# A new hand-written order for the first three batches of an attention and MLP kernel, with one output transfer fewer

## The chip, the cores and the metric

The kernel runs on one core of one Trainium2 chip. The metric is the device time of one execution in microseconds (us). Three runs of the kernel before took 201.86 to 201.91 us, median 201.90 us. The core has five engines with a queue each: PE (TensorE, matrix products), DVE (VectorE), ACT (ScalarE), POOL (GpSimd) and SP (SyncE, which here only issues DMA transfers). ACT and POOL issue a few transfers too.

## The reference

For 8 batches with 8 heads, 512 tokens and 32 state rows of 64 numbers each, attention runs both ways between tokens `x` and rows `state`. The result then goes through two dense layers with a leaky ReLU between them.

```python
scores = scale * x @ state.T;  a  = softmax(scores);  xread = a @ state     # tokens read the states
scores2 = scale * state @ x.T; a2 = softmax(scores2); sread = a2 @ x        # states read the tokens
x = concat([xread, sread], axis=2)            # 8 * 544 rows of 512
out = leaky_relu(x @ w_in, 0.01) @ w_out      # 512 -> 2048 -> 512
```

## The kernel before, in words

The eight batches are worked one behind another, and parts of three of them are in flight at any time. For a batch b these steps occur:

- The tokens are loaded in float32 (`load_x`, tile `xl`, a single buffer), cast to bfloat16 (`cast_x`, tile `xb`) and transposed (tile `xT`). For batch 1 the loads (two tiles `x1`, issued by POOL) are cast on DVE by `cast_x1(u)` and transposed on PE by `turn(u)`, one half u at a time. From batch 2 on `a_xt_dma` transposes by a DMA that SP issues.
- `a_scores` (L223) is a group of eight small products on PE, which needs `xT` and a transposed state. Its result feeds a chain on DVE and ACT: maximum (`a_top`), its spread over rows (`a_rows`), subtraction (`a_less`), exponential (`a_exp`), reciprocal and product (`a_probs`), which gives `aT`. `a_exp2`, `a_max2` and `a_probs2` do the other softmax, `a_a2t` transposes its result by DMA.
- `a_m` (called by `m_make`, and by `mk` in the strings below) multiplies the state by `w_in`, a quarter of the columns at a time, and `m_take` or `ev` copies the result out of PSUM to tile `M`.
- `ff1` (called `ff(j)` or `f.j`) makes one sixteenth of the hidden layer on PE. Its ReLU on ACT (`relu.pop(j)()`, or `r.j`) writes it to `hT`. Two PSUM buffers with the tag `ph` alternate between these, so a later product waits for an earlier ReLU.
- The second layer of batch 0 is cut into `piece(0, h0, i, jq, part=...)`: row group i, quarter jq of the hidden layer, one matmul for each of up to four parts. The pieces of i = 2 and 3 sum in the tile `wide` (named `pyw` in the trace). From batch 1 on the second layer is a fast matrix product with seven products in place of eight (`Fast`), cut into units of two matmuls (`before.run(1)`, or `u`). It needs sums of hidden tiles, made on DVE (`f.sums`, or `sb`, `sn`), and sums of weights, made by `weights_sum` on DVE and POOL into four tiles `tw`.

Nothing is scheduled by a planner. The program runs under `tc.manual_schedule`, so each engine executes its instructions in the order in which the source calls them. For batches 0, 1 and the beginning of 2 the calls stand one by one (L1115 to L1269). For batch 2's own stretch the order is a string of short names, `FIRST` (L1358), which `stretch` (L1270) reads from left to right. Batches 3 to 6 share the string `ORDER`, which stays as it is, and batch 7 has a loop.

A call only fixes the order inside each engine. Waits come from the data: a semaphore wait is put ahead of an instruction whose input or buffer is not ready. The transfers of SP and ACT use eight DMA semaphores in rotation, in the order in which the source calls them, so each transfer also waits until the eighth one before it has landed. At the end of the kernel SP waits for these semaphores one after another, from number 0 to number 7 (shown under L1578), and the cores' engines meet in a barrier.

The names that the change and the prediction touch: on POOL `weights_sum(3, 4, 8)`, `(0, 4, 8)`, `(1, 0, 4)` (L734) and the four casts of batch 3's tokens (L114); on SP the load of batch 3's tokens (L108) and their transposition (L207); on PE the `turn`s (L1095), the pieces (L697), `a_scores` of batches 2 and 3 (L223) and `f.3` of batch 2 (L412); and the output rows of batch 4 in `Batch.done` (L847).

Of the kernel before, what the change touches and what calls it, by code (L numbers as in the profile page):

```python
# [10 lines left out]
B, H, S, D = 8, 8, 512, 64  # L11
# [19 lines left out]
def kernel(  # L31
# [9 lines left out]
    nc = tc.nc  # L41
# [68 lines left out]
    def open_xb(b):  # L110
        xs[b] = xpool.tile([P, NT, H, D] if b < 2 else [P, 2, NT, NK, D], BF16, name="xb", tag="xb")

    def cast_x(b, h0, h1, copy):
        copy(  # L114
            xs[b][:, h0 // NK, :, h0 % NK:h0 % NK + h1 - h0].rearrange("p t h d -> p h t d"),
            xl[b][:, h0:h1].rearrange("p h (t d) -> p h t d", t=NT),
        )
# [59 lines left out]
    def load_state(i, ks=range(NK)):  # L177
        lo, hi = groups[i]
        for k in ks:
            for g in range(2):  # L180
                nc.sync.dma_start(
                    stf[i][NS * k:NS * (k + 1), :, D * g:D * (g + 1)],
                    state[lo:hi, 2 * k + g].rearrange("b n d -> n b d"),
                )
# [10 lines left out]
    def a_open(a, b):  # L195
        a.b = b
        a.xb = xs[b]
        a.xT = att.tile([P, NT, NK, P] if b < 2 else [P, 2, NT, 2, P], BF16, name="xT", tag="xT")
# [108 lines left out]
    def a_exp2(a, g):  # L307
        if g == 0:
            a.e2 = att.tile([P, 2, S], BF16, name="e2", tag="e2", bufs=3)
            a.r2 = att.tile([P, 2], FP32, name="r2", tag="r2", bufs=3)  # L310
        nc.scalar.activation(  # L311
            out=a.e2[:, g], in_=a.sc[:, g, :], func=AF.Exp,
            bias=a.m2[:, g:g + 1], accum_out=a.r2[:, g:g + 1],
        )
# [376 lines left out]
    def piece(b, hT, i, jq, bank=None, copy=SCA, part=range(4)):  # L691
        if jq == 0:
            y = ys[b, i] = Y()
            y.py = psum.tile([P, DM], FP32, name="py", tag="py")[:] if bank is None else bank
        y = ys[b, i]
        for j in (4 * jq + v for v in part):
            nc.tensor.matmul(  # L697
                y.py, lhsT=hT[:, j, P * i:P * (i + 1)], rhs=w_out_bf[:, j, :],
                start=(j == 0), stop=(j == 15),
            )  # L700
        if jq == 3 and copy is not None:
            y_store(b, i, copy)
# [20 lines left out]
    def weights_open():  # L723
        for tag in ("xf0", "xf1", "x10", "x11"):
            tw.append(consts.tile([P, NM, HC], BF16, name=f"tw_{tag}", tag=tag))
# [60 lines left out]
    class Batch:  # L786
# [44 lines left out]
        def done(self, n, bank, copy=SCA):  # L831
            f = self.f
            if n in (1, 6, 5, 7):
                f.save(n, bank, copy)
            if n == 2:
                f.join(self.yo(0)[:, :, :HC], bank, 1)
                if self.b == B - 1:
                    self.out(0, slice(0, HC))
            elif n == 7:
                nc.gpsimd.tensor_tensor(  # L840
                    out=self.yo(1)[:, :, HC:], in0=f.sv[7][:], in1=f.sv[5][:], op=ALU.add
                )
                if self.b == B - 1:
                    self.out(1, slice(HC, DM))
            elif n == 3:
                f.join(self.yo(0)[:, :, HC:], bank, 6)
                for i in range(2) if self.b in (2, 3, 4) else (None,):  # L847
                    self.out(0, slice(HC if self.b == B - 1 else 0, DM), i)
            elif n == 4:
                f.join(self.yo(1)[:, :, :HC], bank, 7)  # L850
                self.out(1)
# [238 lines left out]
    def turn(u):  # L1090
        pt[u] = psum.tile([P, NT, 2, P], BF16, name="pxt2", tag="ph")
        for t in range(NT):
            for v in range(2):
                h = NK * u + 2 * v
                nc.tensor.transpose(  # L1095
                    pt[u][:, t, v, :], a1.xb[:, t, h:h + 2, :].rearrange("p h d -> p (h d)"), ident[:]
                )

    def cast_x1(u):
        VEC(  # L1100
            a1.xb[:, :, NK * u:NK * (u + 1)].rearrange("p t h d -> p h t d"),
            x1[u][:].rearrange("p h (t d) -> p h t d", t=NT),
        )

    def m_make(a, c, tag):
        pmt[a.b, c] = a_m(a, c, tag)
# [8 lines left out]
    h1 = hpool.tile([P, 16, S], BF16, name="hT", tag="hT")  # L1115
    before = Batch(1, h1)
    wide = psum.tile([P, 2, DM], FP32, name="pyw", tag="big", bufs=1)
    a_exp2(a0, 0)
    piece(0, h0, 0, 0)
    load_state(0)  # L1120
    cast_x1(0)
    turn(0)
    cast_x1(1)
    piece(0, h0, 2, 0, bank=wide[:, 0])
    piece(0, h0, 1, 0)
    a_exp2(a0, 1)
    VEC(a1.xT[:, :, 0:2, :], pt[0][:])
    turn(1)
    VEC(a1.xT[:, :, 2:4, :], pt[1][:])
    piece(0, h0, 3, 0, bank=wide[:, 1])  # L1130
    m_make(a1, 1, "ph")
    open_xb(2)
    weights_open()
    a_scores(a1)
    m_take(a1, 1, 0, SCA)
    m_take(a1, 1, 1, VEC)
    a_top(a1)
    piece(0, h0, 0, 1, copy=None, part=(0, 1))
    piece(0, h0, 1, 1, copy=None, part=(0, 1))
    piece(0, h0, 2, 1, copy=None, part=(0, 1))  # L1140
    piece(0, h0, 1, 1, copy=None, part=(2, 3))
    m_make(a1, 2, "ph")
    m_take(a1, 2, 0, SCA)
    m_take(a1, 2, 1, SCA)
    weights_sum(2, 0, 4, nc.gpsimd)
    weights_sum(0, 0, 4, nc.gpsimd)
    state_t(0)
    piece(0, h0, 0, 1, copy=None, part=(2, 3))
    piece(0, h0, 2, 1, copy=None, part=(2, 3))
    piece(0, h0, 3, 1, copy=None, part=(0, 1))  # L1150
    m_make(a1, 3, "ph")
    piece(0, h0, 2, 2, copy=None, part=(0, 1))
    piece(0, h0, 1, 2, copy=None, part=(0, 1))
    a_rows(a1)
    a_less(a1)
    a_exp(a1)
# [2 lines left out]
    cast_x(2, 4, 5, POO)  # L1159
    cast_x(2, 5, 6, POO)  # L1160
    cast_x(2, 6, 7, POO)
    a_open(a2, 2)
    cast_x(2, 7, 8, POO)
    a_probs(a1, 0)
    piece(0, h0, 0, 2, copy=None, part=(0, 1))
    a_xt_dma(a2, slice(1, 2))
    piece(0, h0, 0, 2, copy=None, part=(2, 3))
    piece(0, h0, 3, 1, copy=None, part=(2, 3))
    piece(0, h0, 2, 2, copy=None, part=(2, 3))
    piece(0, h0, 3, 2, copy=None, part=(0, 1))  # L1170
    a_xt_dma(a2, slice(0, 1))
    a_exp2(a1, 0)
    a_probs(a1, 1)
    piece(0, h0, 1, 2, copy=None, part=(2, 3))
    piece(0, h0, 3, 2, copy=None, part=(2, 3))
    load_x(3, nc.sync)
    open_xb(3)
    piece(0, h0, 3, 3, copy=None, part=(0, 1))
    weights_sum(2, 4, 8)
    weights_sum(1, 4, 8)  # L1180
    weights_sum(3, 4, 8, nc.gpsimd)
    weights_sum(0, 4, 8, nc.gpsimd)
    weights_sum(1, 0, 4, nc.gpsimd)
    cast_x(3, 0, 2, POO)
    a_exp2(a1, 1)
    m_take(a1, 3, 0, SCA)
    cast_x(3, 2, 4, POO)
    cast_x(3, 4, 6, POO)
    piece(0, h0, 2, 3, copy=None, part=(0, 1))
    m_make(a2, 0, "sc")  # L1190
    m_take(a1, 3, 1, SCA)
    ff(0)
    ff(1)
    m_take(a2, 0, 0, VEC)
    relu.pop(0)()
    piece(0, h0, 3, 3, copy=None, part=(2, 3))
    m_take(a2, 0, 1, VEC)
    relu.pop(1)()
    ff(2)
    piece(0, h0, 2, 3, copy=None, part=(2, 3))  # L1200
    ff(3)
    relu.pop(2)()
    a_a2t(a0)
    a_scores(a2)
    cast_x(3, 6, 8, POO)
    relu.pop(3)()
    y_store(0, 2, SCA)
    y_store(0, 3, SCA)
    piece(0, h0, 0, 3, copy=None, part=(0, 1))
    piece(0, h0, 0, 3, copy=None, part=(2, 3))  # L1210
    a_top(a2)
    a_open(att_of[3], 3)
    a_rows(a2)
    y_store(0, 0, SCA)
    ff(4)
    a_less(a2)
    ff(5)
# [5 lines left out]
    piece(0, h0, 1, 3, copy=None, part=(0, 1))  # L1223
    ff(9)
    a_a2t(a1)
    a_xt_dma(att_of[3])
    a_max2(a2)
    relu.pop(6)()
    piece(0, h0, 1, 3, copy=None, part=(2, 3))
    relu.pop(8)()  # L1230
    relu.pop(9)()
# [1 line left out]
    a_exp(a2)  # L1233
    a_probs(a2, 0)
    before.run(1)
    a_probs2(a0)
    ff(10, "big")
    before.run(1)
    ff(12)
    relu.pop(10)()  # L1240
    before.run(1)
    ff(13)
    before.run(1)
    before.run(1)
    before.run(1)
    load_state(1, range(2, 4))
    before.f.sums(0, 0, 4)
    a_probs(a2, 1)
    relu.pop(12)()
    relu.pop(13)()  # L1250
    a_exp2(a2, 0)
    a_exp2(a2, 1)
    ff(14)
    relu.pop(14)()
    ff(15)
    relu.pop(15)()
    before.run(1)
    before.run(1)
    before.run(1)
    before.run(1)  # L1260
# [1 line left out]
    m_make(a2, 2, "sc")  # L1262
    m_make(a2, 1, "big")
    m_take(a2, 2, 0, SCA)
    m_take(a2, 1, 0, VEC)
    m_take(a2, 2, 1, SCA)
    before.run(1)
# [2 lines left out]
    def stretch(b, hT, before, now, order):  # L1270
# [85 lines left out]
    )  # L1356

    FIRST = (  # L1358
# [7 lines left out]
    )  # L1366

    for b in range(2, B):
# [4 lines left out]
        if b < B - 1:  # L1373
            stretch(b, hT, before, now, FIRST if b == 2 else ORDER)
            before = now
# [207 lines left out]
```

## Time and profile before

| | |
|---|---|
| median of three runs | 201.90 us (201.86 to 201.91) |
| the profiled execution, its time | 201.93 us |
| its span, first to last instruction | 200.2 us |
| PE busy | 193.9 us (97%), 2090 matmuls |
| DVE, ACT, POOL busy | 164.7, 150.5, 62.2 us |
| TensorE clock granted | 1.00 throughout |
| DMA | 28.02 MB, mean 140 GB/s |

The time of the execution is 1.7 us more than the span: the work around the first and the last instruction. In the profile "busy" of PE is modelled, since matmuls are pipelined. A row of the timeline gives the start, the duration, the engine, the line, the operation, the tiles (output, then inputs) and, in brackets, how long the engine stood idle before it and what ended that. SPq is the issuing of transfers by SP. "DMA to landing" is the time from the start of the issue until the last of the 16 DMA engines has reported the transfer as done.

### The profile page before, as it was taken

Reading aid. Unit: us, or ns where it says so; the run is one execution under the profiler, and the core shown is the slowest. Engines: PE = TensorE matmul, PEld = TensorE weight load, DVE = VectorE, ACT = ScalarE, POOL = GpSimd, SP = SyncE. Lnnn points to the kernel's source line nnn. Section 1 sums busy time; section 2 is a strip of 40 time slices with the busy share of each in tenths; the row PEclk is TensorE's granted clock in tenths of the full one; section 3 lists DMA queues with packets and bytes.
Section 4 is the critical chain, followed back from the end, with each engine's and each line's share of the span. In section 5 each row is a group of like instructions: output and inputs, shape, how many; then the busy total and the mean of one; then the engine's idle time right before and its main releaser. Section 6 shows DMA issues by size and latency. Waiting matters only on the chain.

```text
span 200.2 us, 5119 instructions
## 1 busy us (share of the span) xinstructions
PE 193.9 (97%) x2090; PEld 136.5 (68%) x2090; DVE 164.7 (82%) x283; ACT 150.5 (75%) x287; POOL 62.2 (31%) x90
## 2 busy tenths in 40 slices
PE   7999899999999999999999999999999999999992
PEld 2566544345677667776777777767777788799881
DVE  2676579799998989998999899999899977995622
ACT  3478728699778749996999679987999778767610
POOL 8483266591046013310422040400040024004350
PEclk9999999999999999999999999999999999999999
DMA  6999997999543994734393613080023402210035
GB/s 201 210 207 264 238 296 128 183 282 248 146 147 70 303 285 91 228 151 115 68 246 114 177 34 72 7 258 0 3 83 127 82 0 108 105 56 0 7 98 164
DMA packets 39992, 28.02 MB, mean 140 GB/s; under 512 B 25440, under 2 KB 36832, under 8 KB 39968
## 3 DMA queue, kind: packets, MB, share of 16 engines
q1 hardware_dynamic: 34176, 20.35, 38.1%
q0 software_dynamic: 4960, 6.55, 16.1%
q10 hardware_dynamic: 832, 0.79, 1.2%
q8 instruction: 16, 0.26, 0.6%
q14 instruction: 8, 0.07, 0.1%
HBM read 17.30 MB, written 8.91 MB: 131 GB/s over the span
## 4 chain that ended last, share of the span: by engine, by line
PE 89%; DMA 6%; DVE 1%; POOL 1%; ACT 0%; issue 0%
PE yq L768 43%; PE ph L412 18%; DMA x<-in_x_dram 6%; PE pm L391 4%; PE pyw L697 4%; PE py L697 3%; PE pf L490 3%; PE pl L658 3%; PE yu L768 3%; PE pspin L143 2%; PE pl L579 2%; PE psn L357 1%; PE sc L223 1%; PE phw L425 1%; PE pxt L1095 1%; PE yz L768 0%
## 5 line engine op out<-in xcount | busy, mean ns | idle before, releaser
L418 ACT ACTIVATE hT<-ph 128x512 bf16<-128x512 f32 x84 | 48.9, 609 | 12.3 <-PE ph L412 12.1
L768 PEld LDWEIGHTS <-su 128*128 128x128 bf16 x480 | 46.2, 98 | 12.6 <-ACT hT L418 0.4
L412 PE MATMUL ph<-aT,M 128*128 128x512 bf16 x168 | 47.6, 379 | 0.0
L768 PEld LDWEIGHTS <-hT 128*128 128x128 bf16 x336 | 32.3, 98 | 11.7 <-issue 2.5
L768 PE MATMUL yq<-tw_xf,su 128*128 128x256 bf16 x224 | 30.9, 273 | 0.0
L768 PE MATMUL yq<-w_out_bf,hT 128*128 128x256 bf16 x224 | 29.2, 273 | 0.0
L840 POOL TENSOR_TENSOR yo<-sv,sv 128x512 f32<-128x512 f32 x7 | 9.3, 1329 | 42.6 <-ACT e L311 38.2
L412 PEld LDWEIGHTS <-M 128*128 128x128 bf16 x168 | 16.0, 98 | 7.9 <-issue 1.9
L757 DVE TENSOR_TENSOR su<-hT 128x1024 bf16<-128x1024 bf16 x28 | 19.0, 682 | 2.7 <-ACT hT L418 2.7
L1288 ACT CAST M<-pm 128x512 bf16<-128x512 f32 x31 | 17.3, 599 | 1.4 <-PE pm L391 1.4
L114 POOL CAST xb<-xl 128x512 bf16<-128x512 f32 (+1 forms) x24 | 13.5, 604 | 12.6 <-DMA xl<-in_x_dram 12.6
L777 ACT COPY sv<-yq 128x512 f32<-128x512 f32 x24 | 13.9, 585 | 4.1 <-PE yq L768 4.0
L768 PE MATMUL yq<-tw_x,su 128*128 128x256 bf16 x112 | 16.6, 273 | 0.0
L780 DVE TENSOR_TENSOR yo<-yq,sv 128x512 f32<-128x512 f32 x20 | 13.5, 676 | 2.2 <-PE yq L768 2.2
L768 PE MATMUL yq<-w_out_bf,su 128*128 128x256 bf16 x112 | 15.3, 273 | 0.0
L768 PE MATMUL yq<-tw_x,hT 128*128 128x256 bf16 x104 | 13.9, 273 | 0.0
L311 ACT ACTIVATE e<-sc,mcol 128x512 bf16<-128x512 f32 x16 | 11.1, 698 | 0.0
L670 ACT COPY ls<-pl 128x512 f32<-128x512 f32 x16 | 9.5, 591 | 1.6 <-PE pl L658 1.4
L697 PEld LDWEIGHTS <-hT 128*128 128x128 bf16 x64 | 5.8, 98 | 7.0 <-issue 1.1
L757 DVE TENSOR_TENSOR su<-su,hT 128x1024 bf16<-128x1024 bf16 x14 | 9.6, 687 | 0.2
L305 DVE TENSOR_REDUCE mcol<-sc 128x2 f32<-128x1024 f32 x8 | 9.7, 1215 | 0.0
L1302 POOL COPY after<-mrow 128x1 f32<-128x1 f32 x3 | 0.6, 187 | 28.9 <-DVE mrow L233 28.9
(193 smaller groups left out, 359.9 us busy)
## 6 DMA issues: line engine op xcount, KB each, us to landing
xl<-in_x_dram SPq DMA_DIRECT2D x5, 1024.0 KB, 6.4
out_dram<-yo SPq DMA_DIRECT2D x9, 512.0 KB, 2.9
out_dram<-yo SPq DMA_DIRECT2D x9, 256.0 KB, 2.7
w_in_bf<-in_moe_w_in_dram POOLq DMA_DIRECT2D x4, 512.0 KB, 8.0
w_out_bf<-in_moe_w_out_dram POOLq DMA_DIRECT2D x2, 512.0 KB, 13.5
x<-in_x_dram POOLq DMA_DIRECT2D x2, 512.0 KB, 12.1
w_out_bf<-in_moe_w_out_dram POOLq DMA_DIRECT2D x4, 256.0 KB, 12.6
xl<-in_x_dram POOLq DMA_DIRECT2D x2, 512.0 KB, 15.2
```

What stands on the lines that cost most here:

```text
L114: copy(xs[b][:, h0 // NK, :, h0 % NK:h0 % NK + h1 - h0].rearrange("p t h d -> p h t d"), xl[b][:, h0:h1].rearrange("p h (t d) -> p h t d", ...
L305: nc.vector.tensor_reduce(out=a.m2[:], in_=a.sc[:], axis=AX.X, op=ALU.max, negate=True)
L311: nc.scalar.activation(out=a.e2[:, g], in_=a.sc[:, g, :], func=AF.Exp, bias=a.m2[:, g:g + 1], accum_out=a.r2[:, g:g + 1],)
L412: nc.tensor.matmul(ph[:], lhsT=a.M[:, g, P * j:P * (j + 1)], rhs=a.aT[:, g, :], start=(g == 0), stop=(g == 1),)
L418: nc.scalar.activation(out=hT[:, j, :], in_=ph[:], func=AF.Prelu, scale=1.0 / SCALE, alpha=0.01)
L670: copy(self.sv[n], flat)
L697: nc.tensor.matmul(y.py, lhsT=hT[:, j, P * i:P * (i + 1)], rhs=w_out_bf[:, j, :], start=(j == 0), stop=(j == 15),)
L757: (eng or nc.vector).tensor_tensor(out=S[n][:, ms], in0=u[:, ms], in1=v[:, ms], op=op)
L768: nc.tensor.matmul(bank[:, i, :], lhsT=lhs[:, m, P * i:P * (i + 1)], rhs=rhs[:, m, :], start=(first and m == 0 and (i == 0 or of is not No ...
L777: copy(t[:], bank)
L780: nc.vector.tensor_tensor(out=dst, in0=bank, in1=self.sv[n][:], op=ALU.add)
L1288: copy(t.M[:, g, DM * c:DM * (c + 1)], src[g][:] if isinstance(src, list) else src[:, g, :])
```

## The change

The second `piece` of batch 0 moves ahead of `turn(0)`, and both casts of batch 1's tokens stand ahead of it. `load_state(0)` is called earlier. The later pieces, the copies out of PSUM, the hidden-layer products and their ReLUs of batches 0 to 2 are called in another order, and two copies change engine (`m_take(a2, 0, 0)` from DVE to ACT, `y_store(0, 2)` from ACT to DVE). The call of `load_x(3)` moves up to directly behind the two half transposes of batch 2. On POOL the first cast of batch 3's tokens now stands ahead of the last sum of weights. In `FIRST` the scores `S` stand ahead of `f.3`, `casts` and `turn` stand ahead of `st` or `loads`, and several evictions change place or engine (A is ACT, V is DVE). Batch 4's first output rows leave in one transfer in place of two, which shifts every later transfer by one DMA semaphore. All other work is the same.

```diff
-                for i in range(2) if self.b in (2, 3, 4) else (None,):
+                for i in range(2) if self.b in (2, 3) else (None,):
                     self.out(0, slice(HC if self.b == B - 1 else 0, DM), i)
...
+    load_state(0)
     a_exp2(a0, 0)
     piece(0, h0, 0, 0)
-    load_state(0)
+    piece(0, h0, 1, 0)
     cast_x1(0)
+    cast_x1(1)
     turn(0)
-    cast_x1(1)
     piece(0, h0, 2, 0, bank=wide[:, 0])
-    piece(0, h0, 1, 0)
+    VEC(a1.xT[:, :, 0:2, :], pt[0][:])
     a_exp2(a0, 1)
-    VEC(a1.xT[:, :, 0:2, :], pt[0][:])
     turn(1)
     VEC(a1.xT[:, :, 2:4, :], pt[1][:])
...
     piece(0, h0, 1, 1, copy=None, part=(0, 1))
+    m_make(a1, 2, "ph")
     piece(0, h0, 2, 1, copy=None, part=(0, 1))
-    piece(0, h0, 1, 1, copy=None, part=(2, 3))
-    m_make(a1, 2, "ph")
...
     a_xt_dma(a2, slice(0, 1))
+    load_x(3, nc.sync)
+    open_xb(3)
+    piece(0, h0, 1, 2, copy=None, part=(2, 3))
     a_exp2(a1, 0)
     a_probs(a1, 1)
...
     weights_sum(3, 4, 8, nc.gpsimd)
     weights_sum(0, 4, 8, nc.gpsimd)
+    cast_x(3, 0, 2, POO)
     weights_sum(1, 0, 4, nc.gpsimd)
-    cast_x(3, 0, 2, POO)
     a_exp2(a1, 1)
+    cast_x(3, 2, 4, POO)
+    piece(0, h0, 2, 3, copy=None, part=(0, 1))
+    cast_x(3, 4, 6, POO)
     m_take(a1, 3, 0, SCA)
...
     ff(0)
+    m_take(a2, 0, 0, SCA)
+    relu.pop(0)()
     ff(1)
-    m_take(a2, 0, 0, VEC)
-    relu.pop(0)()
     piece(0, h0, 3, 3, copy=None, part=(2, 3))
     m_take(a2, 0, 1, VEC)
     relu.pop(1)()
     ff(2)
+    relu.pop(2)()
+    ff(3)
     piece(0, h0, 2, 3, copy=None, part=(2, 3))
-    ff(3)
-    relu.pop(2)()
...
-    y_store(0, 2, SCA)
+    y_store(0, 2, VEC)
     y_store(0, 3, SCA)
...
     FIRST = (
-        "f.1 f.0 l4 sb.0.4 u u r.1 u r.0 u f.2 d.1.A sb.2.0 f.3 mk.3.big r.2 S d.2 u u u sb.1.4 "
-        "tp ev.3.0.A r.3 f.4 u rows sb.2.4 u rw sb.3.4 u u u casts.0 casts.2 st u u u casts.4 f.5 "
-        "u ls sb.3.0 u u x2 casts.6 loads a2t turn u u ev.3.1.A d.6.A r.4 r.5 u w3 f.6 u d.5.A "
+        "l4 sb.2.0 u sb.0.4 f.1 u f.0 u u r.1 f.2 r.0 d.1.A mk.3.big ev.3.0.A r.2 S f.3 d.2 u u u "
+        "sb.1.4 tp rows rw sb.3.4 casts.0 sb.2.4 r.3 u f.4 u u u u casts.2 u u u casts.4 u u u "
+        "f.5 u u sb.3.0 ls x2 casts.6 st turn ev.3.1.A d.6.A r.4 w3 r.5 a2t loads f.6 u d.5.A u "
```

The rest of the diff swaps neighbours in the same manner: pieces of batch 0 among themselves, `before.run(1)` against `ff` and `relu` of batch 1, and the second half of `FIRST`.

More of the change, by code (lines that the diff above doesn't have):

```diff
@@ L1117 @@
     wide = psum.tile([P, 2, DM], FP32, name="pyw", tag="big", bufs=1)
+    load_state(0)
     a_exp2(a0, 0)
     piece(0, h0, 0, 0)
-    load_state(0)
+    piece(0, h0, 1, 0)
     cast_x1(0)
+    cast_x1(1)
     turn(0)
-    cast_x1(1)
     piece(0, h0, 2, 0, bank=wide[:, 0])
-    piece(0, h0, 1, 0)
+    VEC(a1.xT[:, :, 0:2, :], pt[0][:])
     a_exp2(a0, 1)
-    VEC(a1.xT[:, :, 0:2, :], pt[0][:])
     turn(1)
     VEC(a1.xT[:, :, 2:4, :], pt[1][:])
+    open_xb(2)
+    weights_open()
     piece(0, h0, 3, 0, bank=wide[:, 1])
     m_make(a1, 1, "ph")
-    open_xb(2)
-    weights_open()
     a_scores(a1)
@@ L1148 @@
     piece(0, h0, 0, 1, copy=None, part=(2, 3))
+    piece(0, h0, 3, 1, copy=None, part=(0, 1))
     piece(0, h0, 2, 1, copy=None, part=(2, 3))
-    piece(0, h0, 3, 1, copy=None, part=(0, 1))
     m_make(a1, 3, "ph")
+    piece(0, h0, 0, 2, copy=None, part=(0, 1))
     piece(0, h0, 2, 2, copy=None, part=(0, 1))
-    piece(0, h0, 1, 2, copy=None, part=(0, 1))
     a_rows(a1)
@@ L1161 @@
     cast_x(2, 6, 7, POO)
+    a_probs(a1, 0)
     a_open(a2, 2)
     cast_x(2, 7, 8, POO)
-    a_probs(a1, 0)
-    piece(0, h0, 0, 2, copy=None, part=(0, 1))
     a_xt_dma(a2, slice(1, 2))
+    piece(0, h0, 1, 1, copy=None, part=(2, 3))
     piece(0, h0, 0, 2, copy=None, part=(2, 3))
     piece(0, h0, 3, 1, copy=None, part=(2, 3))
-    piece(0, h0, 2, 2, copy=None, part=(2, 3))
+    piece(0, h0, 1, 2, copy=None, part=(0, 1))
     piece(0, h0, 3, 2, copy=None, part=(0, 1))
     a_xt_dma(a2, slice(0, 1))
+    load_x(3, nc.sync)
+    open_xb(3)
+    piece(0, h0, 1, 2, copy=None, part=(2, 3))
     a_exp2(a1, 0)
     a_probs(a1, 1)
-    piece(0, h0, 1, 2, copy=None, part=(2, 3))
+    piece(0, h0, 2, 2, copy=None, part=(2, 3))
     piece(0, h0, 3, 2, copy=None, part=(2, 3))
-    load_x(3, nc.sync)
-    open_xb(3)
     piece(0, h0, 3, 3, copy=None, part=(0, 1))
@@ L1182 @@
     weights_sum(0, 4, 8, nc.gpsimd)
+    cast_x(3, 0, 2, POO)
     weights_sum(1, 0, 4, nc.gpsimd)
-    cast_x(3, 0, 2, POO)
     a_exp2(a1, 1)
+    cast_x(3, 2, 4, POO)
+    piece(0, h0, 2, 3, copy=None, part=(0, 1))
+    cast_x(3, 4, 6, POO)
     m_take(a1, 3, 0, SCA)
-    cast_x(3, 2, 4, POO)
-    cast_x(3, 4, 6, POO)
-    piece(0, h0, 2, 3, copy=None, part=(0, 1))
     m_make(a2, 0, "sc")
@@ L1211 @@
     a_top(a2)
+    y_store(0, 0, SCA)
     a_open(att_of[3], 3)
     a_rows(a2)
-    y_store(0, 0, SCA)
     ff(4)
@@ L1225 @@
     a_a2t(a1)
-    a_xt_dma(att_of[3])
     a_max2(a2)
     relu.pop(6)()
+    a_xt_dma(att_of[3])
     piece(0, h0, 1, 3, copy=None, part=(2, 3))
@@ L1235 @@
     before.run(1)
-    a_probs2(a0)
     ff(10, "big")
-    before.run(1)
     ff(12)
     relu.pop(10)()
+    a_probs2(a0)
+    before.run(1)
     before.run(1)
     ff(13)
-    before.run(1)
-    before.run(1)
     before.run(1)
@@ L1249 @@
     relu.pop(12)()
+    before.run(1)
+    before.run(1)
     relu.pop(13)()
@@ L1255 @@
     ff(15)
-    relu.pop(15)()
-    before.run(1)
     before.run(1)
@@ L1264 @@
     m_take(a2, 2, 0, SCA)
+    relu.pop(15)()
+    before.run(1)
     m_take(a2, 1, 0, VEC)
```

8 rows, old and new, of the table FIRST are left out of this document.

## The prediction, made before the changed kernel ran

> **What bounds the kernel now.** I read the page first (the slices and the chain that ended last), then the engines' busy time in stretches of 10 us, then the timeline where PE is not full. In the slices each digit is a fortieth of the span.
>
> ```profile
> PE   7999899999999999999999999999999999999992
> PEclk9999999999999999999999999999999999999999
> ...
> PE 89%; DMA 6%; DVE 1%; POOL 1%; ACT 0%; issue 0%
> ...
> 20.00:30.00 10.00, 9.22 (x80) 4.63 (x79) 6.47 (x8) 4.77 (x11) 4.64 (x4) 1.00 1.16 268
> 30.00:40.00 10.00, 10.00 (x66) 3.99 (x64) 8.81 (x13) 7.45 (x15) 5.93 (x8) 1.00 0.84 155
> 50.00:60.00 10.00, 10.00 (x115) 6.74 (x114) 10.00 (x15) 7.76 (x15) 2.11 (x3) 1.00 0.49 147
> ```
>
> PE bounds it. Its clock is full, the chain is PE for 89% of the span, and from 30 us on PE is busy in all 10.00 of 10 us. The change removes no PE work. It can gain only where PE stands still, which is before 23 us, and behind the last product. It loses wherever it makes PE stand still, since nothing later can win that back.
>
> **The opening.**
>
> ```profile
> 21.11 1.03 PE L697 MATMUL py<-w_out_bf,hT 128*128 128x512 bf16 x4
> 22.16 0.69 DVE L1100 CAST xb<-x 128x1024 bf16<-128x1024 f32 x1 [1.33 <-DMA x<-in_x_dram]
> 22.92 0.62 PE L1095 MATMUL pxt<-ident,xb 128*128 128x128 bf16 x8 [0.78 <-DVE xb L1100]
> 23.59 0.69 DVE L1100 CAST xb<-x 128x1024 bf16<-128x1024 f32 x1 [0.73 <-DMA x<-in_x_dram]
> 24.24 1.03 PE L697 MATMUL py<-w_out_bf,hT 128*128 128x512 bf16 x4
> 25.10 0.61 PE L1095 MATMUL pxt<-ident,xb 128*128 128x128 bf16 x8
> ```
>
> PE idles 0.78 us until the first half of batch 1's tokens has landed and is cast. The piece that ran from 24.24 to 25.10 (0.86 us by the starts) now stands ahead of the first transposes and fills that wait. They still start at 22.92, and the second ones could start at 24.24. Their cast ends at 23.59 + 0.69 = 24.28. With the 0.07 us that lay between cast (22.85) and transposes (22.92) they start at 24.35 instead of 25.10. So PE is 0.75 us early. Bounds: 0.86 if the cast is no limit, 0.6 if the copy of the first transposes takes DVE in between. DVE does the same two casts and copies in the same order, and `load_state` called earlier moves nothing on SP, where it stands behind the same two loads.
>
> **The reordered pieces, copies and ReLUs up to 39 us.** They are the same PE instructions, so the sum is zero unless one waits.
>
> ```profile
> 36.81 1.08 ACT L418 ACTIVATE hT<-ph 128x512 bf16<-128x512 f32 x2 [1.08 <-PE ph L412]
> 39.34 1.25 DVE L233 TRANSPOSE_TENSOR_REDUCE mrow<-sc 128x32 f32<-128x1024 f32 x1 [0.91 <-PE sc L223]
> 33.80 2.61 SPq L207 DMA_TRANSPOSE xT<-xb  x2
> 38.86 0.41 PE L223 MATMUL sc<-xT,st_t 64*32 64x512 bf16 x8
> ...
> L207 SPq DMA_TRANSPOSE xT<-xb x2: 1232/1260/1289, 33.8 to 35.1; - x2
> ...
> DMA to landing us min/median/max: 3.2/3.2/3.2
> ```
>
> The copy that ACT takes over (`m_take(a2, 0, 0)`, about 0.6 us like its neighbours) falls into ACT's idle 1.08 us, and the one that DVE takes over (`y_store(0, 2)`) into DVE's 0.91 us. Without that cover each costs up to 0.6 us. `ff(3)` directly behind `ff(2)` needs the second ReLU's buffer, which comes free just then: I take 0, at most 0.2 us. The scores of batch 2 wait for the second half transpose. It is issued at 35.1 behind POOL's casts, which hang on a load that the change doesn't touch, and lands 3.2 us later, at 38.3. PE would come at 38.86 - 0.75 = 38.11 and starts at about 38.35. The lead shrinks to 0.5 us.
>
> **The moved cast on POOL.** This is the step that decides.
>
> ```profile
> 36.51 0.52 SPq L108 DMA_DIRECT2D xl<-in_x_dram  x1
> ...
> DMA to landing us min/median/max: 6.8/6.8/6.8
> ...
> 37.32 2.12 POOL L734 TENSOR_TENSOR tw_x<-tw_xf,w_out_bf 128x1024 bf16<-128x1024 bf16 x1 [3.55 <-DVE tw_xf L734]
> 39.41 2.12 POOL L734 TENSOR_TENSOR tw_xf<-w_out_bf 128x1024 bf16<-128x1024 bf16 x1
> 41.49 2.12 POOL L734 TENSOR_TENSOR tw_xf<-w_out_bf,tw_x 128x1024 bf16<-128x1024 bf16 x1
> 43.56 2.28 POOL L114 CAST xb<-xl 128x512 bf16<-128x512 f32 x4
> ```
>
> The load of batch 3's tokens is issued at 36.51 and lands at 43.3. It is already next behind batch 2's half transposes on SP, so moving its call changes neither. Before, POOL made three sums of weights meanwhile and then cast. Now the first cast stands ahead of the third sum. With a start 0.75 us earlier POOL has done two sums at 40.8 and waits until 43.3 for the load. Then come one cast (0.6), the sum (2.1) and three casts (1.7): the end is at 47.8 instead of 45.84, 2 us later. Behind the last cast SP holds the transposition of batch 3's tokens, and behind that on SP four more state loads, an output and the next token load.
>
> ```profile
> 45.87 3.13 SPq L207 DMA_TRANSPOSE xT<-xb  x1
> ...
> DMA to landing us min/median/max: 6.2/6.2/6.2
> ...
> 51.00:52.00 1.00, 1.00 (x7) 0.41 (x5) 1.00 (x3) 0.94 (x3) 0.00 (x0) 1.00 0.18 41
> ...
> q8 instruction: 1, 0.02, 0.6%
> ...
> L207 SPq DMA_TRANSPOSE xT<-xb x1: 1761/1761/1761, 76.7 to 76.7; - x1
> ...
> DMA to landing us min/median/max: 4.3/4.3/4.3
> ```
>
> Before, this transposition was issued at 45.87 and landed 6.2 us later, at 52.05. The one issued at 76.7, with nothing queued ahead, took 4.3 us. So part of the 2 us is given back: the queue has drained by then, and 47.8 + 4.3 = 52.1. But the DMA engines were only 0.18 busy from 51 to 52 us, in front of the landing: the last engine was late alone. In the stretch 44 to 53 us the instruction queue q8 holds 0.6% of 16 engines, 0.006 x 16 x 9 = 0.9 us of one engine. PE reaches the same instruction about 0.5 us earlier and so the same load falls again into the transposition. I add 0.9 us: landing at 53.0. Ends: 52.1 with no late engine, 53.9 to 54.0 if it is late by the whole 1.9 us that 6.2 stands above 4.3. I take 0.9, by the row of q8.
>
> **The scores of batch 3.**
>
> ```profile
> 51.14 1.03 PE L412 MATMUL ph<-aT,M 128*128 128x512 bf16 x4
> 52.09 0.41 PE L391 MATMUL pm<-w_in_bf,st_t 64*32 64x512 bf16 x8
> 52.32 0.40 PE L223 MATMUL sc<-xT,st_t 64*32 64x512 bf16 x8
> 53.32 0.59 PE L412 MATMUL ph<-aT,M 128*128 128x512 bf16 x2
> ```
>
> Before, PE came to them at 52.32, 0.3 us behind the landing. Now `S` stands ahead of `f.3` (two matmuls, 0.43 us, half of the four that took 0.86 us from 51.14), and PE has a lead of 0.5 us. It arrives at 52.32 - 0.43 - 0.5 = 51.4, waits for the landing at 53.0 and starts at 53.05. PE has 1.6 us of nothing there, and all behind it stands in one queue. Against before, the scores start 0.73 us late, and `f.3` is still to do: 0.73 + 0.43 = 1.16 us. The lead from the opening is gone; it only lengthened the wait.
>
> **The rest of FIRST and the loads behind.** Same PE work. The scores' chain on DVE and ACT starts no later against PE than before, so the ReLU and copy waits don't grow; I take 0, up to 0.2 us. The later token loads have over a microsecond to spare behind this.
>
> **The end.**
>
> ```profile
> 196.90 0.36 SPq L807 DMA_DIRECT2D out_dram<-yo  x1
> ...
> out_dram<-yo SPq DMA_DIRECT2D x1, 128.0 KB, 1.9
> ...
> L1578 SPq EVENT_SEMAPHORE  x8: 27/28/28, 198.8 to 199.3; - x8
> ```
>
> The last output lands at 196.90 + 1.9 = 198.8. It is on DMA semaphore 0, so SP still has the waits for 1 to 7 ahead of it: eight waits from 198.8 to 199.3, about 0.06 us each. With one transfer fewer in batch 4 the last output is on semaphore 7, and the other seven are passed while it is under way. Gain 7 x 0.06 = 0.43 us, between 0.35 and 0.5. One transfer of 512 KB in place of two of 256 KB costs no engine anything.
>
> **Sum.** Against the profiled execution (201.93 us, 0.03 above the median): +1.16 at batch 3's scores, -0.43 at the end: 202.6 us.
>
> **Rivals.**
> No late engine: the transposition lands at 52.1 and the scores start at 52.15. Then 201.93 - 0.17 + 0.43 - 0.43 = 201.8 us, no change (0.2% is 0.4 us, about what the runs can tell). For it: transpositions issued later in the kernel take 4.3 us. Against it: the landing at 52.05 with idle engines.
> No wait, and faster: if the transposition landed 3.2 us behind its issue, as the half transposes did, it would be there at 51.0, before PE at 51.4. The lead of 0.5 us and the end's 0.43 us would stand: 201.0 us. It decides below 3.6 us of landing. Against it: no full transposition took under 4.3 us. The Trainium skill, DMA: Bandwidth & Descriptors, section Anatomy of one DMA, fits a transfer as about 2.0 us plus bytes over 436 GB/s (measured for POOL's transfers). For this half megabyte an estimate by it is 3.2 us, so by that page this rival would hold; the trace's 4.3 us for the same instruction disagrees, and I go by the trace.
> Worse: the late engine costs the whole 1.9 us (scores at 54.0, 201.93 + 1.7 = 203.6 us), or ReLUs wait too: above 203.4 us.
>
> **Chances.** Late engine (202.2 to 203.4 us) 0.50; no late engine 0.20; no wait 0.20; worse 0.10. Faster is the third, 0.20; the same is the second, 0.20; slower the first and last, 0.60. The range 201.0 to 203.4 us leaves out the last and the half of the third that lies lower; the likeliest's own is 202.2 to 203.4 us.
>
> **What would show it.** PE's idle 0.78 us ahead of the first transposes under 0.1; POOL idle about 2.5 us ahead of a cast at 43.3 and batch 3's transposition issued near 47.8; PE waiting over a microsecond for it at the scores near 53 us; one wait on SP behind the last landing. I am wrong if the load of batch 3's tokens lands by 41 us, if the transposition lands by 51.4, or if PE waits elsewhere.

## The result and the profile after

The changed kernel takes 202.42 us in the median of 15 executions, the kernel before 201.83 us in the median of 15: a ratio of 1.0043, with a 95% interval of 1.0024 to 1.0062. It is slower, by 0.6 us. One execution of 1117 us stands alone and is left aside. The others spread from 202.12 to 203.85 us, while the kernel before stayed within 201.59 to 202.24 us. That spread is part of the story.

The profiled execution of the changed kernel took 202.17 us (span 200.4 us), 0.24 us more than the profiled one of before. In the list of what PE waited for, the 0.8 us at L1095 are gone, and the scores stand first (columns: engine and line, what ended the wait, total, times, longest):

```profile
PE sc L223 <- DMA xT<-xb: 1.2, 2, 1.0
PE pspin L143 <- DVE warm L76: 1.2, 1, 1.2
PE pxth L875 <- DVE xb L121: 0.2, 1, 0.2
```

The timeline of PE, changed kernel, at the places that the prediction named:

```profile
22.85 0.61 PE L1095 MATMUL pxt<-ident,xb 128*128 128x128 bf16 x8
...
24.16 0.61 PE L1095 MATMUL pxt<-ident,xb 128*128 128x128 bf16 x8
...
38.33 0.41 PE L223 MATMUL sc<-xT,st_t 64*32 64x512 bf16 x8 [0.25 <-DMA xT<-xb]
...
51.13 0.41 PE L391 MATMUL pm<-w_in_bf,st_t 64*32 64x512 bf16 x8
52.54 0.41 PE L223 MATMUL sc<-xT,st_t 64*32 64x512 bf16 x8 [1.00 <-DMA xT<-xb]
```

The second transposes start 0.94 us earlier than before (25.10). At batch 2's scores, which wait 0.25 us, 0.53 us of the lead are left (38.33 against 38.86). Batch 3's scores take the rest and more: they start at 52.54 instead of 52.32, with `f.3` still to come. The timeline of POOL and one source line of SP, changed kernel, show why:

```profile
36.50 2.12 POOL L734 TENSOR_TENSOR tw_x<-tw_xf,w_out_bf 128x1024 bf16<-128x1024 bf16 x1 [3.04 <-DVE tw_xf L734]
38.58 2.12 POOL L734 TENSOR_TENSOR tw_xf<-w_out_bf 128x1024 bf16<-128x1024 bf16 x1
42.11 0.61 POOL L114 CAST xb<-xl 128x512 bf16<-128x512 f32 x1 [1.41 <-DMA xl<-in_x_dram]
42.68 2.12 POOL L734 TENSOR_TENSOR tw_xf<-w_out_bf,tw_x 128x1024 bf16<-128x1024 bf16 x1
44.75 1.72 POOL L114 CAST xb<-xl 128x512 bf16<-128x512 f32 x3
```

```profile
L207 SPq DMA_TRANSPOSE xT<-xb x1: 1886/1886/1886, 46.5 to 46.5; - x1
...
  PE sc L223: 1.0, 1
...
DMA to landing us min/median/max: 6.0/6.0/6.0
```

POOL stands idle 1.41 us in front of the moved cast, the casts end at 46.47 instead of 45.84, and the transposition of batch 3's tokens lands 6.0 us after its issue, at 52.5 us.

By batch 4's scores the PE of the changed kernel is 0.65 us late, 0.22 us from the start of batch 3's scores and 0.43 us from `f.3`. The same row in the two timelines, before and then changed:

```profile
72.13 0.41 PE L223 MATMUL sc<-xT,st_t 64*32 64x512 bf16 x8
```

```profile
72.78 0.41 PE L223 MATMUL sc<-xT,st_t 64*32 64x512 bf16 x8
```

At the end SP has one wait in place of eight behind the last landing (waits of L1578 from 199.2 to 199.5 us, changed kernel):

```profile
L1578 SPq EVENT_SEMAPHORE  x1: 28/28/28, 199.5 to 199.5; - x1
```

So in this execution 0.65 - 0.43 = 0.22 us, against 0.24 us measured. The median is 0.6 us above before, though. This execution is one of the fastest of the fifteen, and what the slower ones paid besides is not in this trace, except as a warning. On SP the load of batch 5's tokens now stands directly ahead of batch 1's first output rows, and DVE's first join of batch 2, which writes the same buffer again, waits for that output. SP's and DVE's timelines, changed kernel:

```profile
63.62 1.81 SPq L207 DMA_TRANSPOSE xT<-xb  x1
65.53 1.83 SPq L330 DMA_TRANSPOSE a2T<-e  x1
67.45 0.53 SPq L108 DMA_DIRECT2D xl<-in_x_dram  x1
68.08 1.39 SPq L807 DMA_DIRECT2D out_dram<-yo  x2
```

```profile
75.42 0.69 DVE L780 TENSOR_TENSOR yo<-yq,sv 128x512 f32<-128x512 f32 x1 [0.62 <-DMA out_dram<-yo]
```

Before, the order on SP was the load at 62.30 us, both transpositions and then the output, which landed 3.2 us after its issue, and DVE's join did not wait for it. SP's timeline, DVE's timeline and one source line of SP, kernel before:

```profile
62.30 0.52 SPq L108 DMA_DIRECT2D xl<-in_x_dram  x1
62.91 1.53 SPq L330 DMA_TRANSPOSE a2T<-e  x1
64.53 4.41 SPq L207 DMA_TRANSPOSE xT<-xb  x1
69.03 1.01 SPq L807 DMA_DIRECT2D out_dram<-yo  x2
```

```profile
74.09 0.65 DVE L780 TENSOR_TENSOR yo<-yq,sv 128x512 f32<-128x512 f32 x1
```

```profile
L807 SPq DMA_DIRECT2D out_dram<-yo x1: 532/532/532, 69.0 to 69.0; - x1
...
DMA to landing us min/median/max: 3.2/3.2/3.2
```

In the changed kernel it took 7.3 us. Here PE was not held up by it: the join ended at 76.11 and PE used its bank at 76.83 us. But only 0.7 us lay between.

### The profile page after: what moved, and what is told of

Read it like the earlier page. It is cut to its first block, busy times and chain, and to the rows that moved or that the text cites. A ratio compares the mean times of both kernels' runs of the same rounds, so it can differ in the third digit from the quotient of the medians.

```text
span 200.4 us, 5118 instructions
## 1 busy us (share of the span) xinstructions
PE 194.0 (97%) x2090; PEld 136.5 (68%) x2090; DVE 164.7 (82%) x284; ACT 150.1 (75%) x286; POOL 62.0 (31%) x90
## 4 chain that ended last, share of the span: by engine, by line
PE 86%; DMA 8%; POOL 2%; DVE 1%; ACT 1%; issue 0%; ACTq 0%; SPq 0%
PE yq L768 41%; PE ph L412 15%; PE pm L391 4%; PE pf L490 3%; PE pyw L697 3%; PE pl L658 3%; PE yu L768 3%; DMA xT<-xb 3%; PE ph L1049 3%; DMA xl<-in_x_dram 3%; PE py L697 3%; DMA xf<-in_x_dram 2%; PE pl L579 2%; POOL xb L114 1%; PE psn L357 1%; PE sc L223 1%
## 5 line engine op out<-in xcount | busy, mean ns | idle before, releaser
L114 POOL CAST xb<-xl 128x512 bf16<-128x512 f32 (+1 forms) x24 | 13.0, 581 | 13.8 <-DMA xl<-in_x_dram 13.8
L1288 ACT CAST M<-pm 128x512 bf16<-128x512 f32 x30 | 16.8, 595 | 0.6 <-PE pm L391 0.6
L780 DVE TENSOR_TENSOR yo<-yq,sv 128x512 f32<-128x512 f32 x20 | 13.6, 680 | 4.2 <-PE yq L768 3.6
```

The lines of the kernel that those rows point to most:

```text
L114: copy(xs[b][:, h0 // NK, :, h0 % NK:h0 % NK + h1 - h0].rearrange("p t h d -> p h t d"), xl[b][:, h0:h1].rearrange("p h (t d) -> p h t d", ...
L780: nc.vector.tensor_tensor(out=dst, in0=bank, in1=self.sv[n][:], op=ALU.add)
L1288: copy(t.M[:, g, DM * c:DM * (c + 1)], src[g][:] if isinstance(src, list) else src[:, g, :])
```

## The experiments

The first four ran together, the next four together, and the last three together. Each group had a chip of its own. The kernel before had a median of 201.75, 201.75 and 201.74 us in them, so a ratio to before holds in every group. The changed kernel itself is less steady: it had 202.42 us in the result above and 203.17 us in the second group, and the first group has no run of it. Comparisons with it are therefore firm only inside the second group.

### The third sum ahead of the first cast again

```diff
     weights_sum(0, 4, 8, nc.gpsimd)
-    cast_x(3, 0, 2, POO)
     weights_sum(1, 0, 4, nc.gpsimd)
+    cast_x(3, 0, 2, POO)
```

> The changed kernel with POOL's last sum of weights put back ahead of the first cast of batch 3's tokens. Theory (the moved cast delays the transposition, and PE waits for it at batch 3's scores): the casts end about 45.1 us instead of 46.5, the transposition is issued 1.4 us earlier and lands at about 51.1 where it landed at 52.5, before PE comes (51.4). PE's wait of 1.00 us goes to under 0.1, and the time falls by about 1.0 us, to 201.2, below the kernel before. Rival (POOL's order is indifferent because the DMA queue is the limit): the landing stays at 52.5 and the time within 0.2 us of the changed kernel.

Measured: 201.83 us, ratio to before 0.9997 (0.9977 to 1.0018). The wait at the scores is gone, and the loss against before with it, though the 201.2 us that were expected were not reached. In the profiled execution (201.62 us) the transposition is issued at 45.51 and lands at 51.5 us. But the gain of the opening and of the end does not show either: without its wait of 1.0 us the changed kernel's 202.17 us would be 201.2. DVE's timeline in this run shows the next limit, which had been covered by the scores' wait:

```profile
75.21 0.69 DVE L780 TENSOR_TENSOR yo<-yq,sv 128x512 f32<-128x512 f32 x1 [1.43 <-DMA out_dram<-yo]
```

PE comes earlier now, the output does not, and DVE waits 1.43 us in place of 0.62. From batch 4's scores to batch 5's PE takes 20.98 us here (71.77 to 92.75), where it took 20.48 in the changed kernel (72.78 to 93.26): half of the saved microsecond is lost again in this stretch.

### `f.3` ahead of the scores again

```diff
-        "... r.0 d.1.A mk.3.big ev.3.0.A r.2 S f.3 d.2 u u u "
+        "... r.0 d.1.A f.3 mk.3.big ev.3.0.A r.2 S d.2 u u u "
```

> The changed kernel with the hidden product f.3 put back ahead of batch 3's scores. Theory: the landing is not moved, so 0.43 us of PE work fills the wait: it falls from 1.00 to about 0.55 us and the time by about 0.43 us, to 201.75. Rival (PE's arrival is not what is late, or f.3 waits for a ReLU there): the time stays within 0.15 us of the changed kernel.

Measured: 203.15 us, ratio 1.007 (1.0046 to 1.0094), against 201.75 expected: a miss. The wait at batch 3's scores did shrink, from 1.00 to 0.15 us, yet the time is about that of the changed kernel in the second group (203.17 us, below). What PE waited for in this run:

```profile
...
PE yq L768 <- DVE yo L780: 0.6, 1, 0.6
PE sc L223 <- DMA xT<-xb: 0.4, 2, 0.2
PE pl L658 <- DVE ls L673: 0.2, 1, 0.2
```

The time saved at the scores came back as a wait of PE for DVE's join (L780), that is, for the output. In this execution PE reaches batch 4's scores 0.67 us earlier than in the changed kernel's first profile, and loses 1.1 us on the way to batch 5's (21.56 us in place of 20.48). The output, too, lands 0.7 us later than there (at 76.1).

### Two transfers again

```diff
-                for i in range(2) if self.b in (2, 3) else (None,):
+                for i in range(2) if self.b in (2, 3, 4) else (None,):
```

> The changed kernel with batch 4's first rows leaving in two transfers again, so that the last output is on DMA semaphore 0. Theory: seven waits on SP stand behind the last landing again, 0.43 us more: the stretch from the last landing to the end of the program goes from about 0.9 to 1.35 us, and the time to 202.6. Rival: the semaphore of the last transfer is indifferent, change under 0.1 us.

Measured: 203.64 us, ratio 1.0084 (1.0057 to 1.011): 0.47 us above the changed kernel's 203.17 us of the second group. The two ran in different groups, and the changed kernel's own median moves by more than that between groups, so this shows little. The same part alone on the kernel before, below, is the clean test.

### PE's instruction load moved off the transposition

```diff
-    spin(7, "py")
+    spin(1, "py")
+    nudge = psum.tile([P, S], FP32, name="pnudge", tag="py")
+    for _ in range(60):
+        nc.tensor.matmul(nudge[:4, :4], lhsT=idle[:, :4], rhs=idle[:, :4], start=True, stop=True)
```

This cuts six warm-up products and adds 60 tiny ones to the opening. It changes no output, only how many instructions PE has behind it, and with that the moment at which its next 16 KB of instructions are loaded.

> The changed kernel with six of the seven warm-up products at its start replaced by sixty tiny ones (4x4, their result is not used), 108 PE instructions more. They move the place at which PE's instruction load occurs, and no data. Theory (one of 16 DMA engines carries PE's 16 KB instruction load during batch 3's transposition and is late alone): the load occurs near 45.3 us instead of 50.5, ahead of the transposition, which then lands about 4.4 us behind its issue instead of 6.0, near 51.0, before PE comes. PE's wait goes, time about 201.2. Rival (the engine is late for another reason): the landing stays 6.0 us behind its issue and the time within 0.2 us of the changed kernel.

Measured: 204.57 us, ratio 1.011 (1.0052 to 1.0167). Its profiled execution ran at a granted clock of 0.987 and took 206.5 us, so the transposition alone is read from it; the other five executions took 203.11 to 205.93 us, where 201.2 was expected. PE's instruction load fell at 43.2 us, ahead of the issue at 47.63, and the transposition landed in 4.3 us (SP's source line L207):

```profile
DMA to landing us min/median/max: 4.3/4.3/4.3
```

PE came to the scores without a wait there. In that execution PE waited 2.1 us for the join at L780. That the transposition lands in 4.3 us without the load and in 6.0 us with it in the changed kernel is what the theory forecast, but it is one execution, and its transposition is also issued 1.1 us later. The other runs fill the table. For each, from the trace: the issue of batch 3's transposition, when the 15th and the 16th of the sixteen DMA engines reported it, and when PE's instruction load started, the last three in us behind the issue.

```
run                              issue   15th   16th   load
kernel before                    45.87   4.62   6.18   4.09
before, one transfer             45.89   4.37   5.94   3.85
before, opening                  45.26   4.52   6.08   3.99
changed kernel                   46.50   4.47   5.99   3.97
third sum first                  45.51   4.41   5.97   3.88
two transfers                    46.87   4.47   6.00   4.00
both repairs, first              45.53   4.45   5.98   3.96
both repairs, again              44.96   4.42   6.21   3.91
before, swap                     47.58   5.46   5.47   2.48
changed kernel, again            47.47   5.10   5.14   2.00
f.3 ahead                        47.32   4.89   4.93   1.30
output first                     48.02   4.29   4.31   0.58
instruction load moved           47.63   4.26   4.30  -4.46
```

Where the load starts about 4 us behind the issue, one engine alone is 1.5 to 1.8 us late, eight times of eight. Where it starts sooner or not at all, no single engine is late, five times of five. That bears out the late engine. Over these runs the issue moves by 3.1 us, the landing only from 51.2 to 53.1 us: issued later, the transposition escapes the late engine.

That the instruction load causes the lateness is not shown. The eight transpositions with a late engine are also the eight that were issued before 47.0 us. With the load 0.58 us behind the issue the landing takes 4.3 us, as it does without a load, and as the load starts later the landing of all sixteen grows: 4.9, 5.1 and 5.5 us at 1.3, 2.0 and 2.5 us. And the start of the load itself seems to depend on the transposition. In the changed kernel, its repeat and the run with the output first, PE comes to the scores at 51.5 to 51.9 us, but the load starts at 50.5, 49.5 and 48.6 us: the earlier, the later the transposition was issued.

### The changed kernel again

No edit.

> The changed kernel as it is, as the yardstick of the other three. Expected 202.2 to 202.6 us, with single executions up to 203.9 us. The theory for these: DVE's first join of batch 2 (L780, at 75.4 us) waits for batch 1's first output rows, which now stand behind the 1 MB load of batch 5's tokens on SP and land 7 to 8 us after their issue; in the profiled execution that wait is 0.62 us and PE has some 0.7 us of slack behind it, so a landing a little later reaches PE. The rival: the spread has nothing to do with that output.

Measured: 203.17 us (202.94 to 204.37), ratio 1.0079 (1.0059 to 1.0099). This time the profile caught an execution of 204.37 us, in which the output holds PE up. The first rows of what PE waited for, and DVE's timeline:

```profile
PE yq L768 <- DVE yo L780: 1.6, 1, 1.6
PE pspin L143 <- DVE warm L76: 1.2, 1, 1.2
PE sc L223 <- DMA xT<-xb: 1.0, 2, 0.8
...
```

```profile
77.96 0.69 DVE L780 TENSOR_TENSOR yo<-yq,sv 128x512 f32<-128x512 f32 x1 [3.04 <-DMA out_dram<-yo]
```

The two profiled executions of this one kernel differ by 2.2 us. PE loses 2.1 us of that between batch 4's scores and batch 5's (22.60 us in place of 20.48), and 1.6 us of it is this wait. Its cause can be followed back on POOL, which here gets batch 4's tokens 1.4 us later:

```profile
59.57 2.79 POOL L114 CAST xb<-xl 128x512 bf16<-128x512 f32 x4 [12.12 <-DMA xl<-in_x_dram]
```

In the first profile that row starts at 58.13. Behind these casts SP holds the transposed state, two transpositions, the load and then the output, which is issued at 69.59 in place of 68.08 and lands 8.3 us later. The load of these tokens was issued 0.4 us later (52.7 in place of 52.3) and took 6.7 us to land in place of 5.7. So a token load that lands a little late moves the whole row of transfers, and the last of them now ends PE's slack.

### The output ahead of the load

```diff
-        "... turn ev.3.1.A d.6.A r.4 w3 r.5 a2t loads f.6 u d.5.A u "
-        "... f.10 u u d.3 r.11 "
+        "... turn ev.3.1.A d.6.A r.4 w3 r.5 a2t f.6 u d.5.A u "
+        "... f.10 u u d.3 loads r.11 "
```

> The changed kernel with the load of batch 5's tokens called behind batch 1's first output rows (d.3) in place of two transfers ahead of them. Theory (the output behind the load is the second limit): the output lands by 73 us, 3 to 4 us earlier, DVE's wait of 0.62 us at L780 goes, single executions above 203 us go, and the median comes down to 202.2 us or a little less, 0.2 to 0.3 us below the changed kernel; the 1.0 us wait of PE at batch 3's scores stays. Rival (the output is hidden anyway): the same median and the same spread as the changed kernel.

Measured: 202.37 us (201.85 to 202.71), ratio 1.0022 (1.0011 to 1.0033): 0.8 us below the changed kernel beside it, and nothing above 203 us. The output lands 3.8 us behind its issue in place of 8.3, and DVE's join runs at once, in an order that is otherwise the changed one (SP's timeline, its line L807, and DVE's timeline):

```profile
68.69 0.53 SPq L807 DMA_DIRECT2D out_dram<-yo  x1
69.31 0.39 SPq L108 DMA_DIRECT2D xl<-in_x_dram  x1
```

```profile
DMA to landing us min/median/max: 3.8/3.8/3.8
```

```profile
74.56 0.65 DVE L780 TENSOR_TENSOR yo<-yq,sv 128x512 f32<-128x512 f32 x1
```

PE takes 20.47 us from batch 4's scores to batch 5's, as before. The theory held, and the gain was larger than it expected. The kernel is still 0.62 us slower than the kernel before, and PE still waits 0.87 us at batch 3's scores.

### Both repairs

The third sum ahead of the cast, and the output ahead of the load. It ran in the second group and once more in the third.

> Both repairs together: on POOL the third sum of weights ahead of the first cast again (as in the first experiment, 201.83 us), and the load of batch 5's tokens behind batch 1's first output rows. Theory (the wait that the repaired scores handed on is that for the output, which held DVE 1.43 us at 75.2 us in the first experiment, and PE lost some 0.4 us by 86 us): 201.3 us, 0.4 to 0.5 us below the first experiment, and below the kernel before. Rival (the output is hidden, and the first experiment's lead went elsewhere): 201.8 us as in the first experiment.

> The kernel with both repairs (third sum ahead of the first cast, load of batch 5's tokens behind batch 1's first output rows) a second time, since its median of 201.09 us rests on few executions: 201.0 to 201.3 us again, faster than the kernel before by 0.2 to 0.4%.

Measured: 201.09 us (200.99 to 201.25, five executions), ratio 0.9966 (0.9953 to 0.9979), and 201.25 us (200.79 to 203.35, twelve), ratio 0.9981 (0.9961 to 1.0001). In the second group that is 1.28 us below the run with the output alone repaired: the moved cast costs more there than the output. This is the fastest version here, though the second interval just touches no change. In the profiled execution of 200.79 us PE waits for nothing but its own start; the whole list is:

```profile
PE pspin L143 <- DVE warm L76: 1.2, 1, 1.2
```

### One part alone on the kernel before

The end: only the one transfer in place of two, `self.b in (2, 3)`.

> The kernel before with nothing changed but batch 4's first output rows in one transfer. Theory: the last output is on the last of the eight semaphores, seven waits of 0.06 us are passed while it is under way, 0.35 to 0.5 us less: 201.3 us against 201.75. Rival (the waits are hidden by the work around the last instruction, or the larger transfer costs as much): 201.75 us, no change.

Measured: 201.30 us (201.10 to 201.63), ratio 0.9978 (0.997 to 0.9987), that is 0.45 us less. As expected.

The swap: only the first cast ahead of the third sum, on POOL.

> The kernel before with one edit: on POOL the first cast of batch 3's tokens ahead of the third sum of weights. Nothing of the opening, of FIRST or of the end is changed. Theory (the swap is what delays the transposition): two sums end at 41.6 us, the cast waits for the load, which lands at 42 to 43.3 us, the casts end at 46.5 to 47.8 us, the transposition lands 6.0 us behind its issue at 52.5 to 53.8 us, and PE, which comes to the scores at 52.32 us, waits 0.2 to 1.5 us: 202.0 to 203.2 us. Rival (PE is late enough in this order, with f.3 ahead of the scores, to be untouched): 201.75 us.

Measured: 202.54 us (202.38 to 202.78), ratio 1.0032 (1.002 to 1.0044), 0.80 us more. PE's timeline shows it at one place, 0.77 us behind the 52.32 of before:

```profile
53.09 0.41 PE L223 MATMUL sc<-xT,st_t 64*32 64x512 bf16 x8 [0.47 <-DMA xT<-xb]
```

The opening: only the second piece ahead of `turn(0)`.

```diff
     load_state(0)
+    piece(0, h0, 1, 0)
     cast_x1(0)
     turn(0)
     cast_x1(1)
     piece(0, h0, 2, 0, bank=wide[:, 0])
-    piece(0, h0, 1, 0)
```

> The kernel before with the second piece of batch 0 ahead of the first transposes of batch 1, and nothing else. PE's wait of 0.78 us at 22.9 us goes and PE leads by 0.75 us. Theory (the lead is eaten by the transpositions that PE meets later, whose times hang on loads and not on PE): 0.25 us go at batch 2's scores at 38.3 us, and the transposition of batch 3's tokens, which landed at 52.05 us with PE at 52.32, leaves only 0.2 to 0.3 us: 201.45 to 201.6 us. Rival (the lead is kept to the end): 201.0 us.

Measured: 201.64 us, ratio 1.0001 (0.9987 to 1.0014): 0.1 us less by the medians, within what can be told from nothing. PE's timeline:

```profile
24.23 0.62 PE L1095 MATMUL pxt<-ident,xb 128*128 128x128 bf16 x8
...
38.51 0.41 PE L223 MATMUL sc<-xT,st_t 64*32 64x512 bf16 x8 [0.44 <-DMA xT<-xb]
...
51.97 0.40 PE L223 MATMUL sc<-xT,st_t 64*32 64x512 bf16 x8
```

The lead of 0.87 us (25.10 less 24.23) is 0.35 us at batch 2's scores (38.86 before) and still at batch 3's (52.32 before), where PE does not wait. In this execution the half transposes of batch 2, whose casts wait for a load, eat most of the gain, batch 3's transposition eats none of it, and the 0.35 us stay to the end (201.58 us against 201.93 in the profile of before). The medians do not show them.

## Why the prediction was right, and where it was not

The sign, the time (202.6 us predicted, 202.42 measured) and the range were right. The sum came out partly by luck, because errors had opposite signs: in the first profile the scores cost less than forecast, and the wait for the output was not forecast at all.

- The opening: predicted 0.75 us, in the profile 0.94. The first transposes start 0.07 us earlier than before, and the second ones 0.19 us earlier than estimated, so the gain lies a little above the upper bound of 0.86 us.
- Batch 2's scores at 38.35 us: measured 38.33. Right.
- The moved cast on POOL: the mechanism was right, and the swap alone cost 0.80 us. Its term was mis-sized in this execution: the load landed at 42.1 us instead of 43.3, so the casts ended at 46.47 instead of 47.8. In six other profiled executions with the moved cast it landed between 42.4 and 43.2 us, nearer to the forecast; one row of before is one draw of a load that varies by over a microsecond.
- The landing: 53.0 us predicted, 52.5 measured. The late engine came as forecast, but at 1.5 us in place of 0.9: the share of the queue q8 was the wrong row for its size, and the excess of 6.2 over 4.3 us, which the prediction kept as the upper bound, the nearer one. And the two terms are not independent. With the casts as late as predicted the late engine does not occur, as the table shows.
- Batch 3's scores: +1.16 us predicted. In the profile it is 0.65, of which `f.3` is the 0.43 us predicted and the rest 0.22 in place of 0.73.
- "The rest of FIRST and the loads behind", 0 to 0.2 us: this step failed. The prediction looked at when the later token loads are needed and not at what stands behind them on SP. Its own sign of being wrong, that PE waits elsewhere, appears in the second profile. Batch 1's output is queued behind the load of batch 5's tokens, it is the next user of a buffer for DVE, and DVE's join frees PE's bank. That cost 0 us in one profiled execution and 1.6 us in the other, and putting the output first gave 0.8 us in the median.
- The end: -0.43 us predicted; 0.45 measured alone. In the two traces the span ends 1.33 us behind the last landing before (198.82 to 200.15) and 0.91 us in the changed kernel (199.45 to 200.36), 0.42 us less.

So in the first profiled execution 1.16 - 0.43 was in truth 0.65 - 0.43 at the steps named. That execution is a favourable one. In the second group the kernel with the output first, which has the named steps alone, is 0.62 us above before in the median, near the 0.73 us of the prediction's sum, and the output, which no step had, adds 0.80 us. How the 0.6 us of the first measurement divide between the two was not measured. Of the rivals, the one without a wait is ruled out by the waits of 1.0 and 0.8 us in the two profiles. The one without a late engine is half true: the first profile has the late engine, the second has not, but there the transposition, issued at 47.47 us, lands 5.1 us later and not 4.3, and PE waits all the same. The Trainium skill, DMA: Bandwidth & Descriptors, section Anatomy of one DMA, has the fit for POOL's transfers from which the prediction worked out its estimate of 3.2 us for the transposition. The trace does not bear that out for this transfer of SP, even where nothing disturbs it: 4.3 us.

What stays open: why the changed kernel had a median of 202.42 us in one measurement and 203.17 in another, both beside 201.8 for before. The wait for the output differs between executions and could explain the direction, but how often it occurs was not measured, and the chip may have a part in it. The trace also doesn't name the DMA engine that was late, so that it is the one with PE's instruction load is borne out by timing only, and which of the two delays the other is not settled.

## What to carry to other kernels

When a transfer is moved in a queue, list what is now behind it and who reuses those buffers: an output that nobody reads is waited for by the next writer of its tile. A wait that is removed often uncovers a second one of nearly the same size, so look for the next limit in the run where the first is gone. And a lead gained early is only worth what the fixed times behind it, here the landings of loads, leave of it.

## What the hardware showed unexpectedly

An output of 512 KB that was issued 0.6 us behind a load of 1 MB on the same queue landed 7.3 to 8.3 us after its issue, and 3.8 us when issued 0.6 us ahead of it. In the profile of the changed kernel the load landed 6.7 us after its issue, at 74.1, and the output at 75.4 us, behind it. The six profiles with the output behind the load have 7.3 to 8.3 us, the three with it ahead 3.8. The Trainium skill, DMA: Bandwidth & Descriptors, section Queues, rings and completion order, says that each DMA engine takes the descriptors of one queue in order, and that the write which reports a transfer lands only after every earlier write of that engine; the order of the two landings agrees.

The transposition's lateness goes with where in it PE's instruction load starts: 1.5 to 1.8 us of one engine when it starts 3.9 to 4.1 us behind the issue, none of one engine alone at 0.6 to 2.5 us. The Trainium skill, same page, section Latency and other measured facts, says that the DMA engines 7 and 15 are usually slower than the others. By that two reports should come late in most runs; here it is one in eight of thirteen runs and none in five, so the trace does not bear that out as the cause.
